# In-place weight forms of the 15-product scheme, handed out one operation at a time on GpSimd

## The chip, the cores and the metric

The kernel runs on one core of one Trainium2 chip. The metric is the device time of one execution in microseconds (us), as the median over runs. Each engine of the core takes its instructions in its own order: TensorE (PE in the profile) for matrix products, VectorE (DVE), ScalarE (ACT), GpSimd (POOL), and SyncE (SP), whose queue issues transfers. Engines wait for each other through semaphores.

## The reference

All data are float32. First an attention block: for each of 4 x 8 heads a state of 48 x 48 runs over 768 positions. Then its output, as 3072 rows of 384, goes through a gated feed-forward block:

```python
cur = einsum('bhd,bhe->bhde', u[None] * kt, vt)
y[:, :, t] = einsum('bhd,bhde->bhe', rt, state + cur)
state = w[None, :, :, None] * state + einsum('bhd,bhe->bhde', kt, vt)
...
g = x @ w_gate                               # (3072, 384) @ (384, 1536)
silu = g * (1.0 / (1.0 + exp(-g)))
return (silu * (x @ w_val)) @ w_out          # (3072, 1536) @ (1536, 384)
```

## The kernel before, in words

**Stages.** The attention block works on 24 tiles of 128 positions (six stretches of each of four batches). Its outputs, transposed, land in a ring of ten tiles, `xT`. The feed-forward block takes them in groups `g` of two tiles, and the hidden dimension of 1536 in 12 blocks `f` of 128. The first groups use plain products (`gate_value`, L444). Groups 2 to 7 are taken in pairs with `four` (L590): gate and value of a block, over two groups, come from eleven products of 128 x 128 by 128 x 256 in place of twelve. These use sums of weights made by `w_sums` (L576, five GpSimd operations for two blocks). Groups 8 to 11 are taken in pairs too, by `three_units` (L802), which handles three blocks (a triple `t`) at once with fifteen products.

**The forms.** The fifteen products of a triple need fifteen combinations ("forms") of its weights. Three are made in place, overwriting blocks of the weights `wgv`: `in_place` (L700) issues six GpSimd operations, two for each. A further six are made in other room by `w_forms` (L712), nine operations and a step `place` that names the room. As the weights are overwritten, a triple's in-place forms may begin only when the pair of groups 6 and 7, the last that uses them plainly (`g + 2 == THREES`, with `THREES` at 8), is done with those blocks.

**What sets the order.** All orders are written out by hand; instructions stand on each engine as the program emits them. `four_units` (L640) sorts the steps of a pair by a place, `11 * f - 5 + at`, and cuts them into 26 pieces. A block's steps are: PE products into two accumulator banks (`c_a`, `c_b`); ACT copies of the first bank at three points, named p1, u2 and u3 (L629); DVE sums and products with the second bank (L631 to L638); sigmoids on ACT (L602); and at the end, in step `h1`, one product on DVE (L605) and one on GpSimd (L606), which uses u3 and so gives its buffer back. The copies p1, u2 and u3 live in one ring of six buffers (tag `part`). As the program is built, p1 of block f + 3 takes the buffer that u3 of block f leaves: the copy of p1 on ACT waits for L606 three blocks earlier, and PE waits for the copy, because its next product is added onto the same bank.

`feed` (L872) draws these pieces between the steps of the attention tiles, in the loop of L1004. Each tile `s` brings to GpSimd `scale` (L301 and L304, written into `hats`) and `own_product` (L228 and L229), and at tiles past 12 also `move_blocks` (L349), 16 transfers on SP's queue which read `hats` and which the next tile's L304 has to wait for, and `turn_blocks` (L369), two transposes on DVE (L373) before them. `two_projections` (L656) gives the second product of the feed-forward block for a pair in 14 items; with the pair 6, 7 each item also calls `prepare_threes` (L774), which makes forms of triples 3, 1 and 0. Forms of triples 2 and 3 follow within `three_units`. After the last tile `x_forms` (L744) makes the corresponding sums of the inputs on DVE.

Of the kernel before, what the change touches and what calls it, by code (L numbers as in the profile page):

```python
# [22 lines left out]
def fast(  # L23
# [44 lines left out]
    dve, pool, act, pe, sp = nc.vector, nc.gpsimd, nc.scalar, nc.tensor, nc.sync  # L68
# [210 lines left out]
    for l in range(7):  # L279
        n = 1 << l  # L280
        f = pw[:, :, P - n : P - n + 1].to_broadcast([P, HP, n])
# [294 lines left out]
    def w_sums(g, f):  # L576

        (w11, w12, w13), (w21, w22, w23) = (
            [w[:, c, P * f : P * (f + 2)] for c in range(CC)] for w in (wg, wv)
        )  # L580
        t = three.tile([P, 5, 2 * P], FP32, name="s", tag="w_bits")
        x = part_of.setdefault(g, {})
        x["s", f] = x["s", f + 1] = t
        pool.tensor_add(t[:, 0], w21, w22)
        pool.tensor_sub(t[:, 1], t[:, 0], w11)
        pool.tensor_sub(t[:, 2], w22, t[:, 1])
        pool.tensor_sub(t[:, 3], w12, t[:, 1])
        pool.tensor_sub(t[:, 4], w13, w23)
# [51 lines left out]
    def four_units(g):  # L640

        steps = sorted((11 * f - 5 + at, f, what) for f in range(FC) for what, at in PLACE.items())
        pieces = [[] for _ in range(26)]
        n = 0
        for at, f, what in steps:
            k = max(n - 1, 0) if n < 4 else 3 + min(23 * (n - 4) // (11 * FC - 4), 22)
            if what == "p1" and f % 2 == 0 and f + 2 < FC:
                pieces[k].append(lambda f=f: w_sums(g, f + 2))
            k = (0, 1, 2, 2)[n] if n < 4 else k
            pieces[k].append(lambda f=f, what=what: four(g, f, what))  # L650
            if g + 2 == THREES and what == "h1" and f % 3 == 2 and f < 11:
                pieces[k].append(lambda f=f: in_place(f // 3))
            n += what[0] in "pc"
        return [lambda q=q: [do() for do in q] for q in pieces]

    def two_projections(g):  # L656

        def item(j, p):
            if g >= THREES and (j, p) == (0, 1):
                for do in wide.pop("last"):  # L660
                    do()
            if (j, p) in ((1, 0), (0, 1)):
                h_sums(g, p)
            elif (j, p) in ((1, 1), (0, 3)):
                h_sums(g + 1, p // 3)
            elif g + 2 < THREES:
                if (j, p) == (1, 2):
                    w_sums(g + 2, 0)
                elif (j, p) == (0, 6):
                    x_sums(g + 2)  # L670
            if THREES <= g + 2 < N // 2:
                prepare_threes(g + 2, order.index(f"{j}{p}"))
            project(g + j, p)
        order = "00 10 01 02 11 04 03 12 05 06 13 14 15 16".split()
        return [lambda j=int(o[0]), p=int(o[1]): item(j, p) for o in order]


    THREES = 8
# [19 lines left out]
    wide, todo_forms = {}, deque()  # L698

    def in_place(t):  # L700

        f = 3 * t
        w = [[wgv[:, :, c, P * (f + i) : P * (f + i + 1)] for c in range(CC)] for i in range(3)]
        for o, a, b, op in (
            (w[1][1], w[0][1], w[1][2], pool.tensor_add),
            (w[0][0], w[1][0], w[0][2], pool.tensor_add),
            (w[2][2], w[2][0], w[1][2], pool.tensor_sub),
        ):
            op(o, o, a)
            pool.tensor_sub(o, o, b)  # L710

    def w_forms(t):  # L712

        f = 3 * t
        made = wide["u", t] = {}

        w = [[wgv[:, :, c, P * (f + i) : P * (f + i + 1)] for c in range(CC)] for i in range(3)]
        def place():
            if t == 0:
                ring = three.tile([P, 6, 2, P], FP32, name="s", tag="w_bits")  # L720
                s = [ring[:, n] for n in range(6)]
            else:
                s = (early + spare)[6 * t - 6 : 6 * t]
                s = [x.rearrange("p (o t) -> p o t", o=2) for x in s]
            made.update(zip(("r2", "r3", "r13", "r11", "r5", "r9"), s))
            made.update({
                "r0": w[1][1], "r1": w[0][1], "r4": w[0][0], "r6": w[1][2], "r7": w[2][2],
                "r8": w[1][0], "r10": w[2][0], "r12": w[0][2], "r14": w[2][1],
            })

        def form(o, a, b, op):
            op(made[o], made[a], made[b])

        return [place] + [
            lambda x=x: form(*x) for x in (
                ("r2", "r14", "r6", pool.tensor_sub), ("r3", "r8", "r1", pool.tensor_sub),
                ("r13", "r12", "r10", pool.tensor_add), ("r9", "r2", "r13", pool.tensor_sub),
                ("r9", "r9", "r7", pool.tensor_sub), ("r5", "r3", "r13", pool.tensor_sub),
                ("r5", "r5", "r4", pool.tensor_sub), ("r11", "r3", "r2", pool.tensor_sub),
                ("r11", "r11", "r0", pool.tensor_add),  # L740
            )
        ]

    def x_forms(g):  # L744

        (x00, x01), (x10, x11), (x20, x21) = x_halves(g)
        lows2 = [two.tile([P, 3, 2, P], FP32, name="xf", tag="w_low") for _ in range(2)]
        v = [t[:, n] for t in lows2 for n in range(3)]
        v += [
            t[:].rearrange("p h d -> p (h d)")[:, 0 : 2 * P].rearrange("p (i t) -> p i t", i=2)  # L750
            for t in r_ld + k_ld
        ]
        last = two.tile([P, H, D], FP32, name="xf", tag="rk")
        v.append(
            last[:].rearrange("p h d -> p (h d)")[:, 0 : 2 * P].rearrange("p (i t) -> p i t", i=2)
        )
        v10, v14, v6, v13, v2, v12, d1, v3, v1, v8, v4 = v
        dve.tensor_add(v10, x01, x21)
        dve.tensor_add(v14, x10, x20)
        dve.tensor_sub(v13, x00, v10)  # L760
        dve.tensor_add(v12, v13, x20)
        dve.tensor_sub(d1, x11, x10)
        dve.tensor_sub(v2, d1, x20)
        dve.tensor_add(v6, v2, x21)
        dve.tensor_sub(v3, x00, x11)
        dve.tensor_sub(v1, x10, x00)
        dve.tensor_sub(v8, x01, x11)
        dve.tensor_sub(v4, x01, x00)
        wide["v", g] = {
            "r0": d1, "r1": v1, "r2": v2, "r3": v3, "r4": v4, "r5": x00, "r6": v6, "r7": x21,  # L770
            "r8": v8, "r9": x20, "r10": v10, "r11": x11, "r12": v12, "r13": v13, "r14": v14,
        }

    def prepare_threes(g, n):  # L774
        if g > THREES:
            if n == 10:
                x_forms(g)
            return
        if n == 1:
            in_place(3)  # L780
            todo_forms.extend(w_forms(1))
        if n == 7:
            todo_forms.extend(w_forms(0))
        for _ in range(2):
            if todo_forms:
                todo_forms.popleft()()
# [93 lines left out]
    def queue(g):  # L880
        if g == 0:
            todo.extend(
                (2 * f2 + 2 if j + f else 0, lambda j=j, f=f: gate_value(j, f))
                for f2 in range(FC // 2) for j in range(2) for f in (2 * f2, 2 * f2 + 1)
            )
        elif g % 2 and g > 1:
            first, *others = two_projections(g - 3)
            if g - 1 >= THREES:
                if g - 1 == THREES:
                    todo.extend((NW + 4, x) for x in others)  # L890
                return
            *pieces, last = four_units(g - 1)

            then = two_projections(g - 1)[0]

            for k in range(3):
                others.insert(len(others) - 3 + k, pieces.pop(0))
            pieces = ([first] if g == 3 else []) + others + pieces + [then, last]
            todo.extend((NW + 4, x) for x in pieces)
# [575 lines left out]
```

## Time and profile before

| what | value |
|---|---|
| median of three runs | 621.92 us (621.46 to 623.23) |
| the profiled execution: its time | 621.22 us |
| its span | 619.5 us |
| PE busy | 601.7 us, 97% of the span |
| DVE, POOL, ACT busy | 396.8, 324.7, 234.7 us |
| granted clock of PE | 0.999 |
| in-place forms (L709 and L710) | 24 operations, the first at 372.8 us, the last at 429.2 us |
| one of them | 0.72 to 1.45 us, most 0.73 to 0.76 |
| other forms (L732) | 36 operations from 429.8 to 487.7 us |

The span runs from the first to the last recorded instruction on the core; the execution's own time is 1.7 us more, with what lies around it. Starts in a timeline are microseconds from the span's start. A line such as "L606" is a line of the kernel; what stands left of an arrow is written, what stands right is read; "[3.58 <-POOL hTs L606]" means that the engine was idle for 3.58 us until that instruction released it.

### The profile page before, as it was taken

The numbers are of one execution on the slowest core, as the hardware profiler recorded it, in microseconds if no ns is written. First come the engines' busy times: TensorE is split into PE (matmuls) and PEld (weight loads), VectorE is DVE, ScalarE is ACT, GpSimd is POOL, SyncE is SP. The second block draws the span as 40 slices with busy tenths as digits, with TensorE's granted clock in tenths as the row PEclk, the third lists the DMA queues.
The fourth block names the chain that finished last, engine by engine and source line by source line (L and its number), as shares of the span: only waits on it lengthen the run. The fifth ranks groups of instructions, "written<-read, shape, count | busy, mean of one in ns | idle before, by whom it ended". The sixth has DMA issues, their size and how long they took to land.

```text
span 619.5 us, 12800 instructions
## 1 busy us (share of the span) xinstructions
PE 601.7 (97%) x4992; PEld 541.5 (87%) x4992; DVE 396.8 (64%) x749; ACT 234.7 (38%) x599; POOL 324.7 (52%) x366
## 2 busy tenths in 40 slices
PE   8799999999999999999999999899999999999996
PEld 7588888899888899988899988789988889988896
DVE  6878997364556564556658365659368875478770
ACT  3368786322343522244331334342223331133310
POOL 4789788944638423664633847957725610012200
PEclk9999999999999999999999999999999999999999
DMA  7989882343331203322221502022000000100001
GB/s 174 227 212 248 238 280 46 64 70 62 73 66 26 44 10 69 74 47 40 44 44 37 114 3 46 16 39 31 26 26 2 0 1 12 40 1 1 2 2 55
DMA packets 138006, 40.45 MB, mean 65 GB/s; under 512 B 128592, under 2 KB 131792, under 8 KB 137936
## 3 DMA queue, kind: packets, MB, share of 16 engines
q1 hardware_dynamic: 134480, 34.82, 26.4%
q10 hardware_dynamic: 3456, 4.72, 2.2%
q8 instruction: 41, 0.67, 0.5%
q14 instruction: 29, 0.24, 0.1%
HBM read 28.51 MB, written 4.72 MB: 54 GB/s over the span
## 4 chain that ended last, share of the span: by engine, by line
PE 78%; POOL 7%; SPq 3%; DVE 3%; DMA 2%; issue 1%; ACT 1%; DVEq 0%; POOLq 0%; ACTq 0%
PE o_f L522 13%; PE c_b L622 10%; PE c_l L797 10%; PE c_a L622 9%; PE o_a L522 8%; PE gv L448 7%; PE o_b L522 6%; PE y_ps L411 4%; PE c_y L797 3%; PE c_n L797 3%; SPq L358 3%; PE s_ps L381 3%; POOL wgv L216 1%; DMA hats<-hats 1%; POOL hTs L606 1%
## 5 line engine op out<-in xcount | busy, mean ns | idle before, releaser
L448 PE MATMUL gv<-xT,wgv 128*128 128x256 f32 x288 | 66.8, 385 | 0.6 <-ACT xT L415 0.6
L322 ACT ACTIVATE At<-ident,du 128x128 f32<-128x128 f32 x176 | 61.0, 396 | 15.2 <-DVE o_sb L536 7.2
L622 PE MATMUL c_b<-xT,wgv 128*128 128x256 f32 x216 | 64.5, 380 | 0.0
L821 POOL TENSOR_TENSOR At<-At,hats 128x512 f32<-128x512 f32 x8 | 10.2, 1272 | 97.9 <-ACT At L820 97.9
L448 PEld LDWEIGHTS gv<-xT,wgv 128*128 128x128 f32 x288 | 53.3, 190 | 8.8 <-ACT xT L415 0.9
L606 POOL TENSOR_TENSOR hTs<-hTs,u 128x256 f32<-128x256 f32 x36 | 27.9, 774 | 51.3 <-DVE hTs L605 51.0
L622 PE MATMUL c_a<-t,s 128*128 128x256 f32 x144 | 43.7, 385 | 2.9 <-ACT p L629 2.9
L622 PEld LDWEIGHTS c_b<-xT,wgv 128*128 128x128 f32 x216 | 40.8, 190 | 5.3
L386 DVE COPY_PREDICATED At<-mask,s_ps 128x512 f32<-128x512 int32 x48 | 33.0, 741 | 18.0 <-PE s_ps L381 9.5
L629 ACT COPY u<-c_a 128x256 f32<-128x256 f32 x72 | 26.7, 370 | 45.8 <-PE c_a L622 44.4
L622 PE MATMUL c_a<-xT,wgv 128*128 128x256 f32 x144 | 42.9, 379 | 0.0
L602 ACT ACTIVATE sg<-hTs 128x256 f32<-128x256 f32 x72 | 29.9, 416 | 30.2 <-DVE hTs L631 21.4
L304 POOL TENSOR_TENSOR hats<-r_ld,scales 128x384 f32<-128x384 f32 x20 | 21.0, 1049 | 32.0 <-DMA hats<-hats 32.0
L622 PE MATMUL c_b<-xT,s 128*128 128x256 f32 x144 | 37.0, 379 | 0.0
L636 DVE TENSOR_TENSOR u<-u,c_b 128x256 f32<-128x256 f32 x36 | 15.0, 417 | 33.1 <-PE c_b L622 29.6
L411 PE MATMUL y_ps<-At,v_ld 128*32 128x128 f32 x768 | 34.9, 273 | 1.3 <-DVE At L386 1.3
L622 PEld LDWEIGHTS c_a<-t,s 128*128 128x128 f32 x144 | 26.6, 190 | 7.6 <-ACT p L629 4.1
L411 PEld LDWEIGHTS y_ps<-At,v_ld 128*32 128x32 f32 x768 | 30.3, 110 | 2.4 <-issue 1.4
L631 DVE TENSOR_TENSOR hTs<-p,c_b 128x256 f32<-128x256 f32 x36 | 15.0, 417 | 24.8 <-PE c_b L622 22.3
L622 PEld LDWEIGHTS c_b<-xT,s 128*128 128x128 f32 x144 | 27.2, 190 | 3.9
L622 PEld LDWEIGHTS c_a<-xT,wgv 128*128 128x128 f32 x144 | 27.3, 190 | 3.5
L411 PE MATMUL y_ps<-rT,Z 112*32 112x128 f32 x480 | 29.8, 276 | 0.3 <-ACT kT L347 0.3
(241 smaller groups left out, 1528.3 us busy)
## 6 DMA issues: line engine op xcount, KB each, us to landing
hats<-hats SPq DMA_DIRECT2D x192, 32.0 KB, 2.0
w_bits<-in_moe_w_gate_dram SPq DMA_DIRECT2D x6, 768.0 KB, 6.7
v_ld<-in_v_dram SPq DMA_DIRECT2D x48, 96.0 KB, 3.3
w_bits<-in_moe_w_val_dram SPq DMA_DIRECT2D x6, 768.0 KB, 6.2
w_bits<-in_moe_w_out_dram SPq DMA_DIRECT2D x6, 768.0 KB, 6.4
out_dram<-o_sb ACTq DMA_DIRECT2D x24, 192.0 KB, 2.0
k_ld<-in_k_dram SPq DMA_DIRECT2D x20, 192.0 KB, 3.0
r_ld<-in_r_dram SPq DMA_DIRECT2D x20, 192.0 KB, 4.1
```

The source lines that it names most:

```text
L304: pool.tensor_mul(rhat_of(i)[:, :, 0:D], raw(i)[1], rscale)
L322: lambda h=h: act.activation(At[i % 2][:, h, :], ident[:], AF.Identity, scale=du[:, h : h + 1])
L358: sp.dma_start(out=bass.AP(tensor=dst.tensor, offset=dst.offset, ap=[list(dst.ap[0]), [-P, 2 * HP], [1, 32]],), in_=bass.AP(tensor=src.ten ...
L386: dve.copy_predicated(At[i % 2][:].rearrange("p (a e) t -> p a e t", e=2)[:, :, e], mask[:].bitcast(INT32).unsqueeze(1).to_broadcast([P, H ...
L411: pe.matmul(ps[32 * q : 32 * q + 32, cc, :], *x, start=start, stop=stop, skip_group_check=True,)
L448: pe.matmul(gv[:, o, :].rearrange("p (i t) -> p i t", i=2), wt[:, c, P * f : P * (f + 1)], xT[:, 2 * g % NX : 2 * g % NX + 2, c, :], start ...
L522: pe.matmul(ps, lhs[:, f, :], rhs[:, f, :], start=(f == 0 and n in (0, 1, 4)), stop=(f == FH - 1), skip_group_check=True,)
L602: act.activation(x[what, f][:], h[j], AF.Sigmoid)
L606: pool.tensor_mul(h[1], h[1], x.pop(("u3", f))[:])
L622: pe.matmul(ps.rearrange("p (i t) -> p i t", i=2), lhs, rhs, start=first, stop=what not in ("p2", "p5", "p4", "p3"), skip_group_check=True,)
L629: act.copy(x[nm, f][:], ps)
L797: pe.matmul(wide[chain][:, o].rearrange("p (i t) -> p i t", i=2), u[:, o], v, start=first and o == 0, stop=True, skip_group_check=True,)
```

## The change

`in_place` now returns its six operations as a list instead of issuing them, in the same order within each pair. For triples 0, 1 and 2 `four_units` gives each operation a place of its own: `11 * f + 20 + 5.4 * m` for the m-th of the triple that ends with block f, where all six stood behind `h1` of that block before (whose place is `11 * f + 19.5`). Two thus come to each following block. They go into the piece that the step ahead of them went to. For triple 3 the six go to the front of the list `todo_forms`, from which each item of the projections draws two, where all six were issued with item 1 before. Item 7 puts the forms of triple 0 ahead of what is left of triple 1's, where they followed it before.

The operations, their shapes and the buffers that they use stay as they are. The order of PE, DVE, ACT and SP stays as it is. On GpSimd, by the built order, L606 of blocks 2 to 11 of the pair stand in this row ("2x" are two in-place operations, "sums" one call of `w_sums`, "tile" L301, L304, L228 and L229 of one attention tile):

```
before: b2 6x b3 sums b4 b5 6x tile sums b6 L439 L439 b7 tile b8 6x b9 b10 b11 6x ...
after:  b2 2x b3 2x sums b4 2x b5 2x tile sums b6 1x L439 L439 1x b7 1x tile 1x b8 2x b9 2x b10 2x b11 6x ...
```

Another ring buffer changes hands: the copy of the first partial product of the projection (L530) now waits for L606 of block 9, for which the copy of its u2 (L530 too) waited before.

```diff
@@ four_units
         steps = sorted((11 * f - 5 + at, f, what) for f in range(FC) for what, at in PLACE.items())
+        if g + 2 == THREES:
+            steps += [
+                (11 * f + 20 + 5.4 * m, f, do)
+                for f in (2, 5, 8) for m, do in enumerate(in_place(f // 3))
+            ]
+            steps.sort(key=lambda x: x[0])
         pieces = [[] for _ in range(26)]
         n = 0
         for at, f, what in steps:
+            if not isinstance(what, str):
+                pieces[k].append(what)
+                continue
             k = max(n - 1, 0) if n < 4 else 3 + min(23 * (n - 4) // (11 * FC - 4), 22)
...
             pieces[k].append(lambda f=f, what=what: four(g, f, what))
-            if g + 2 == THREES and what == "h1" and f % 3 == 2 and f < 11:
-                pieces[k].append(lambda f=f: in_place(f // 3))
             n += what[0] in "pc"
@@ in_place
-        for o, a, b, op in (
-            (w[1][1], w[0][1], w[1][2], pool.tensor_add),
-            (w[0][0], w[1][0], w[0][2], pool.tensor_add),
-            (w[2][2], w[2][0], w[1][2], pool.tensor_sub),
-        ):
-            op(o, o, a)
-            pool.tensor_sub(o, o, b)
+        return [
+            lambda o=o, x=x, op=op: op(o, o, x) for o, x, op in (
+                (w[1][1], w[0][1], pool.tensor_add), (w[1][1], w[1][2], pool.tensor_sub),
+                (w[0][0], w[1][0], pool.tensor_add), (w[0][0], w[0][2], pool.tensor_sub),
+                (w[2][2], w[2][0], pool.tensor_sub), (w[2][2], w[1][2], pool.tensor_sub),
+            )
+        ]
@@ prepare_threes
         if n == 1:
-            in_place(3)
-            todo_forms.extend(w_forms(1))
+            todo_forms.extend(in_place(3) + w_forms(1))
         if n == 7:
-            todo_forms.extend(w_forms(0))
+            todo_forms.extendleft(reversed(w_forms(0)))
```

## The prediction

> **What bounds the kernel now.** I read the page's busy shares first. TensorE (PE) is busy 97% of a 619.5 us span and no other engine is above 64%, so a change on GpSimd (POOL) can only move the end through PE's idle time. The next view is the waits, of PE and of ScalarE (ACT), longest first; the columns are us in total, times, longest.
>
> ```profile
> PE c_a L622 <- ACT p L629: 2.9, 3, 2.2
> ACT p L629 <- POOL hTs L606: 7.4, 4, 3.6
> ```
>
> PE's longest wait anywhere is 2.2 us, for ACT's copy of p1 (L629). ACT in turn waited up to 3.6 us for L606, GpSimd's last step of a block. The timelines (start, us, engine, line) show that these are one event. ACT's:
>
> ```profile
> 396.01 0.37 ACT L629 COPY u<-c_a 128x256 f32<-128x256 f32 x1 [0.42 <-PE c_a L622]
> 396.37 0.42 ACT L602 ACTIVATE sg<-hTs 128x256 f32<-128x256 f32 x1
> 400.37 0.37 ACT L629 COPY p<-c_a 128x256 f32<-128x256 f32 x1 [3.58 <-POOL hTs L606]
> 401.54 0.37 ACT L629 COPY u<-c_a 128x256 f32<-128x256 f32 x1 [0.79 <-PE c_a L622]
> 403.26 0.37 ACT L629 COPY u<-c_a 128x256 f32<-128x256 f32 x1 [0.35 <-PE c_a L622]
> ```
>
> and PE's at the same moment:
>
> ```profile
> 397.97 0.59 PE L622 MATMUL c_b<-xT,wgv 128*128 128x256 f32 x2
> 400.80 0.70 PE L622 MATMUL c_a<-t,s 128*128 128x256 f32 x2 [2.24 <-ACT p L629]
> ```
>
> Counting blocks, the copy at 400.37 is p1 of block 9 of group pair 6 (the u at 396.01 is u3 of block 8, at 403.26 u3 of block 9). An undisturbed block takes 4.75 us from u3 to u3 (378.46, 383.21, 387.95 in the same timeline); here it took 403.26 - 396.01 = 7.25. So the wait costs PE 7.25 - 4.75 = **2.50 us**, a little more than the idle 2.24, because the pipeline restarts slowly.
>
> Why L606 was late is in the chain of waits, which leaves PE at 385.34 and comes back at 400.80:
>
> ```profile
> 386.20 0.73 POOL hTs L606
> 386.93 0.70 POOL wgv L709
> ...
> 391.66 0.97 POOL hats L301
> 392.63 0.97 POOL hats L304
> ...
> 395.63 0.70 POOL s L584
> ...
> 399.66 0.69 POOL hTs L606
> ```
>
> From L606 of block 5 to L606 of block 6 GpSimd never rests: six in-place forms, four operations for the attention tile, five weight sums, then L606. Ahead of it, at 382.98 to 386.20, it sat idle for 3.22 us, waiting for VectorE (DVE) to finish L605 of block 5.
>
> **What the Trainium skill says.** "Perfetto Trace Analysis", section "Optimization Strategy", says to take the gaps of the engine that counts and ask which semaphore ended each; this trace answers with the chain above. The same section reads a gap that repeats as too few buffers; here 2.2 of PE's 2.9 us on this wait are one gap, so it is one piece of queueing and not the ring of six in general. "SBUF — State Buffer", section "Who interferes with whom", says that a DVE instruction with two SBUF inputs and a GpSimd instruction that reads SBUF block each other. The trace agrees: L709 takes 0.72 to 0.73 us mostly, and 1.44 at 422.73, while DVE runs the sums of L495 to L499. "GPSIMD Engine Reference", section "3.1 Elementwise", gives 2.6 cycles per element for two inputs; for 256 elements at 1.2 GHz that is an estimate of 0.55 us before dispatch. The trace's 0.73 us is used.
>
> **The change, part by part.** Operations on GpSimd: 24 in-place and 36 other forms, the same before and after, of the same shape. Nothing is added or removed, on any engine or queue. Only the order in GpSimd's queue moves, and every other engine keeps its own order.
>
> *Triple 0.* Before, all six forms stood between L606 of blocks 2 and 3. Now two follow each of blocks 2, 3 and 4. After block 2's L606 (372.15) two forms end at 374.4; L606 of block 3 still waits for DVE's L605, about 376.6; two forms and five sums follow (two forms 1.5, five sums 4.06), so L606 of block 4 starts at about 382.9, where it was 382.25. P1 of block 7 needs it and is copied at 384.56: 0.9 us to spare. Two forms then run to 385.1, inside what was the idle 3.22 us, so L606 of block 5 stays at 386.20.
>
> *Triple 1.* Two forms follow block 5, in place of six: 386.88 to 388.39. Six took 391.62 - 386.88 = 4.74, two take 1.51, so all behind starts **3.23 us** sooner. The attention operations have their inputs, and the rows before and after show no wait on them in the queue. L606 of block 6 starts at 399.62 - 3.23 = 396.39 and ends at 397.1. The copy of p1 of block 9 follows u3 of block 8 by 1.35 us when nothing holds it (378.46 to 379.81), so at 397.36. PE can take it until 398.40 (397.97 plus the pitch of 0.43), thus a copy that starts up to 397.97. There is 0.8 us of spare: the wait goes, with all its 2.50 us.
>
> *The other four of triple 1* follow around L606 of blocks 6 and 7. Block 7's L606 starts at about 399.75 (form, two L439 of 1.15 together, form), and p1 of block 10 is due at 404.61 - 2.50 = 402.1. Hidden by 1.6 us.
>
> *Past the moves of hats.* One form comes ahead of L301, and one behind L229. L304 waits there for the 16 moves on SP's queue. They start at 397.32 on DVE's transpose of 396.59, which lies ahead of the stall and doesn't move; so this wait still ends at 409.35, while PE is 2.50 sooner. What is queued behind L304: L228, L229, one form, L606 of block 8, which ends at 409.35 + 0.95 + 1.08 + 0.96 + 0.75 + 0.75 = 413.85. ACT's u3 of block 11 waits for it and is due at about 413.4, so it is 0.3 to 0.5 late. PE wants that bank next for p4 of block 11, at 418.71 - 2.50 = 416.2, and the copy is done by 414.3: 1.9 us of cover. Then two forms and L606 of block 9 (416.1), which now releases the first projection's p1 copy, due at 418.54 - 2.50 = 416.04. If ACT is held there some tenths, next behind are diagonals and a sigmoid due at 418.6; the o_a bank itself is wanted at 424.7.
>
> *Triple 3 and the forms of triple 0.* Triple 3's six forms follow at two per projection, then five forms for triple 1, then all of triple 0's, then the last four. Triple 0's wait, as before, for the projection that ends at 441.1 (now 438.6), run 9 x 0.745 to 445.3, and are wanted at 458.39 - 2.50. The last four end at 448.3; GpSimd's next work waits for PE at 452.76 - 2.50 = 450.3. Cost nothing; cover 2.0 us.
>
> Sum: -2.50 us and nothing given back. The profiled execution, span 619.5 and time 621.22, would become 617.0 and 618.72. The median of the three runs, 621.92, stands 0.70 above that execution, so the median becomes **619.4**.
>
> The unknown is how much the forms and DVE stretch each other in the new overlaps. Low end: nothing, or a gain, since DVE's L605 of block 10 and two transposes hold PE 0.27 us at 415.80 and that could vanish (619.1). High end: the nine operations between 388.39 and 396.4 each take 0.91 for 0.73, as L588 did beside DVE: 9 x 0.18 = 1.6, so L606 ends 398.7, 0.8 past PE's limit (620.2). I take no stretch, because the same nine ran beside DVE work before and their 8.0 us already hold two stretched sums.
>
> **The rivals.** *A part is given back* (620.5): the stretch above, or later. DVE's x sums (L758 to L764) already hold PE 1.1 us at 457.45, because five of them take 0.84 to 0.96 beside GpSimd; if GpSimd's forms run 1.4 us longer than I have it, L758 and L759 stretch by 0.5 each too. *No change* (621.9): another release becomes the one that ends last. Nearest are p1 of block 7 (0.9 us) and u3 of block 11 (1.9 us); for it to hold, one estimate must be off by over 3 us, while PE, ACT and DVE otherwise keep their order. *Slower* (624): L606 of block 8 is held behind L304 while PE has moved on. It starts to cost once it ends after 415.75, 1.9 us later than worked out, and makes the kernel slower than before by 0.3% only past 415.75 + 2.50 + 1.87 = 420.1. For that the moves must land 6.3 us later than now; they have no new work ahead of them on SP. Against it: issue took 10.41 us and the wait ended 1.6 after.
>
> **How the numbers follow.** Forecast 74%, with its own range 618.6 to 620.2 (the low end above, and the scatter of the runs, 621.46 to 623.23, around their median); given back in part 12%; no change 8%; slower 6%. Of this kernel 0.3% is 1.87 us, about what its measurement tells from no change. The forecast clears that by 0.6 us, so I leave an eighth of it in "same", with most of the second case and all of the third: faster 0.68, same 0.26, slower 0.06. The range, 618.5 to 621.2, takes in the first two cases.
>
> **What would show it.** Right: PE's longest wait for p1 gone and its total for that pair near 0.7 us; ACT's copy of p1 of block 9 at about 397.4; six forms no longer in one run before about 420; L304 still ending its wait at about 409.3; the 1.1 us wait for L764 still there, 2.5 us sooner; span near 617.0. Wrong: a PE wait over 1 us for another copy between 384 and 420, L606 of block 6 later than 397.9, or a last wait at L764 grown to 2 us.

## The result, and the profile after

| | before | after |
|---|---|---|
| median of six runs each | 621.69 us (620.38 to 623.79) | 617.93 us (616.92 to 618.77) |
| the profiled execution: its time | 621.22 us | 618.37 us |
| its span | 619.5 us | 616.6 us |

The ratio is 0.9934, with a 95% interval of 0.9913 to 0.9956: 3.76 us less, where 2.5 had been forecast. The time fell just below the range, whose low end was 618.5. Repeated later, beside 27 runs of the kernel before on the same chip (median 620.98), it was 617.24 (617.04 to 618.45): 0.9946, 0.9929 to 0.9963, or 3.74 us less.

The waits of PE in the changed kernel, longest first (total, times, longest):

```profile
PE warm L263 <- POOL ident masks.py:199: 2.8, 1, 2.8
PE y_ps L411 <- DVE At L386: 1.4, 2, 1.2
PE c_l L803 <- DVE xf L771: 1.1, 1, 1.1
...
PE c_a L622 <- ACT p L629: 0.7, 2, 0.4
```

The wait of 2.2 us for the copy of p1 is gone from the pair in the last row; what is left of it is two of at most 0.4, in total the 0.7 that was forecast. The wait on DVE's x sums (L764 before, L771 now) is still 1.1. The queue that caused the old wait now reads so (GpSimd's timeline, changed kernel; start, us):

```profile
382.67 0.72 POOL L606 TENSOR_TENSOR hTs<-hTs,u 128x256 f32<-128x256 f32 x1
383.36 1.53 POOL L712 TENSOR_TENSOR wgv<-wgv 128x256 f32<-128x256 f32 x2
386.11 0.73 POOL L606 TENSOR_TENSOR hTs<-hTs,u 128x256 f32<-128x256 f32 x1 [1.22 <-DVE hTs L605]
386.80 1.53 POOL L712 TENSOR_TENSOR wgv<-wgv 128x256 f32<-128x256 f32 x2
388.28 1.01 POOL L301 TENSOR_TENSOR hats<-k_ld,scales 128x384 f32<-128x384 f32 x1
...
396.32 0.74 POOL L606 TENSOR_TENSOR hTs<-hTs,u 128x256 f32<-128x256 f32 x1
...
409.90 1.00 POOL L304 TENSOR_TENSOR hats<-r_ld,scales 128x384 f32<-128x384 f32 x1 [7.49 <-DMA hats<-hats]
...
413.83 0.73 POOL L606 TENSOR_TENSOR hTs<-hTs,u 128x256 f32<-128x256 f32 x1
```

The rows of L606 are blocks 4, 5, 6 and 8. Behind block 5 stand two forms (L712, the old L709 and L710) where there were six, and block 6 starts at 396.32 where it was 399.62. Triple 0's forms fill part of the idle time ahead of block 5: 1.22 us is left of 3.22. ACT's timeline, changed kernel, shows what that releases:

```profile
395.87 0.37 ACT L629 COPY u<-c_a 128x256 f32<-128x256 f32 x1 [0.42 <-PE c_a L622]
396.24 0.42 ACT L602 ACTIVATE sg<-hTs 128x256 f32<-128x256 f32 x1
397.22 0.37 ACT L629 COPY p<-c_a 128x256 f32<-128x256 f32 x1 [0.57 <-PE c_a L622]
398.89 0.37 ACT L629 COPY u<-c_a 128x256 f32<-128x256 f32 x1 [1.30 <-PE c_a L622]
400.62 0.37 ACT L629 COPY u<-c_a 128x256 f32<-128x256 f32 x1 [0.35 <-PE c_a L622]
...
414.59 0.37 ACT L629 COPY u<-c_a 128x256 f32<-128x256 f32 x1 [1.37 <-POOL hTs L606]
```

The copy of p1 of block 9 is at 397.22, in place of 400.37, and what ended the idle time before it is PE's own product, no longer GpSimd. From u3 of block 8 to u3 of block 9 it is 400.62 - 395.87 = 4.75 us, the undisturbed pitch.

**Where the time went, in the two traces.** Executions differ by 1 to 2 us before the change's place is reached: PE's wait for `kT` (L347) near 58 us ends anywhere between 57.65 and 59.57 in ten traces, and the copy of u3 of block 7 starts anywhere between 386.26 and 388.15, with the same work ahead of it on PE. So stretches are compared from one fixed event, the copy of u3 of block 7. Spans are known to 0.1 us, so a stretch to the end is good to 0.05.

| from u3 of block 7 to | before | after | difference |
|---|---|---|---|
| u3 of block 9 | 15.31 | 12.80 | -2.51 |
| the first o_a of the projections | 28.38 | 25.54 | -2.84 |
| the c_l behind the x sums | 69.50 | 66.65 | -2.85 |
| the end of the span | 231.55 | 228.78 | -2.77 |

The 2.51 is the wait. The next 0.33 comes at the end of the pair, where DVE held PE in the kernel before (its L605 of block 10 takes 0.75 us there and 0.42 in the changed kernel); PE's timeline of the kernel before,

```profile
415.09 0.60 PE L622 MATMUL c_a<-t,s 128*128 128x256 f32 x2
415.80 0.70 PE L622 MATMUL c_b<-t,s 128*128 128x256 f32 x2
```

and of the changed one:

```profile
412.45 0.59 PE L622 MATMUL c_a<-t,s 128*128 128x256 f32 x2
412.88 0.64 PE L622 MATMUL c_b<-t,s 128*128 128x256 f32 x2
```

The distance falls from 0.71 to the usual 0.43 us. The change need not be what does this: with the forms of triple 2 in one run as before, two traces below show 0.51 (projections alone) and 0.43 (wait filled), and with them spread one shows 0.64 (four ahead). Everything behind stays as it was, to 0.1 us. So the traces hold 2.8 us; the medians differ by 3.75. The remaining 0.9 to 1.0 us is no stretch of these two traces, and the experiments had to find it.

### The profile page after: what moved, and what is told of

Read it like the earlier page. It is cut to its first block, busy times and chain, and to the rows that moved or that the text cites. A ratio compares the mean times of both kernels' runs of the same rounds, so it can differ in the third digit from the quotient of the medians.

```text
span 616.6 us, 12802 instructions
## 1 busy us (share of the span) xinstructions
PE 601.6 (98%) x4992; PEld 541.4 (88%) x4992; DVE 395.5 (64%) x749; ACT 235.0 (38%) x599; POOL 325.4 (53%) x366
## 4 chain that ended last, share of the span: by engine, by line
PE 83%; DMA 4%; SPq 3%; POOL 3%; DVE 3%; ACT 2%; issue 1%; ACTq 0%; DVEq 0%; POOLq 0%
PE o_f L522 13%; PE c_b L622 11%; PE c_l L803 10%; PE c_a L622 10%; PE gv L448 8%; PE o_a L522 8%; PE o_b L522 6%; PE y_ps L411 5%; PE c_y L803 3%; PE c_n L803 3%; PE s_ps L381 3%; SPq L358 3%; DMA w_bits<-in_moe_w_gate_dram 1%; DMA w_bits<-in_moe_w_val_dram 1%; PE u_ps L426 1%
## 5 line engine op out<-in xcount | busy, mean ns | idle before, releaser
L606 POOL TENSOR_TENSOR hTs<-hTs,u 128x256 f32<-128x256 f32 x36 | 28.5, 791 | 48.6 <-DVE hTs L605 48.4
L304 POOL TENSOR_TENSOR hats<-r_ld,scales 128x384 f32<-128x384 f32 x20 | 21.2, 1061 | 33.0 <-DMA hats<-hats 33.0
L439 POOL TENSOR_TENSOR Z<-Z,w 48x192 f32<-48x192 f32 x32 | 18.7, 583 | 22.2 <-DVE Z L438 21.0
```

What stands on the lines that cost most here:

```text
L304: pool.tensor_mul(rhat_of(i)[:, :, 0:D], raw(i)[1], rscale)
L439: pool.tensor_mul(ze, ze, w)
L606: pool.tensor_mul(h[1], h[1], x.pop(("u3", f))[:])
```

## The experiments

The theory is the prediction's: six forms in one run ahead of block 6's L606 delay one copy, PE loses 2.5 us, and nothing else of the change counts. The first rival is that the gain comes from spreading in general: GpSimd's forms meet less of DVE's work, and the two stretch each other less. The second is that the other half of the change, the new order of the forms in the projections, has a part. The first four kernels ran beside 27 runs of the kernel before, median 620.82.

In the table the first two columns are the stretches of the table above, from each trace.

| kernel | u3 of block 7 to u3 of block 9 | to the end | median, us | ratio to before (95%) |
|---|---|---|---|---|
| before | 15.31 | 231.55 | 620.82, 620.98 | |
| spread alone | 12.80 | 228.68 | 617.40 | 0.9950 (0.9932 to 0.9969) |
| projections alone | 16.98 | 232.97 | 620.83 | 1.0003 (0.9993 to 1.0013) |
| one L606 on DVE | 12.80 | 228.84 | 616.93 | 0.9942 (0.9924 to 0.9960) |
| triple 1 alone | 12.81 | 228.65 | 617.29 | 0.9947 (0.9928 to 0.9966) |
| four ahead | 13.78 | 229.86 | 618.19 | 0.9959 (0.9942 to 0.9975) |
| x sums earlier | 12.81 | 227.85 | 616.43 | 0.9929 (0.9913 to 0.9945) |
| wait filled | 15.31 | 231.19 | 619.78 | 0.9984 (0.9976 to 0.9991) |
| after, again | 12.81 | 228.75 | 617.24 | 0.9946 (0.9929 to 0.9963) |

**The two halves of the change.** First the spread in `four_units` alone, with the projections' forms in the old order:

```diff
@@ prepare_threes, against the changed kernel
         if n == 1:
-            todo_forms.extend(in_place(3) + w_forms(1))
+            for do in in_place(3):
+                do()
+            todo_forms.extend(w_forms(1))
         if n == 7:
-            todo_forms.extendleft(reversed(w_forms(0)))
+            todo_forms.extend(w_forms(0))
```

> The forms of triples 0, 1 and 2 are spread as in the changed kernel; in the projections the six of triple 3 stand together with item 1 and triple 0's forms follow triple 1's, as before. Theory (PE waited 2.5 us for p1 of block 9, held by L606 of block 6 behind six forms): all of the gain is here, span about 616.6 like the changed kernel (before 619.5), no PE wait for p1 over 0.5 us. Rival (part of the gain beyond the 2.5 us forecast comes from the new order in the projections): span 617.0 or more, gain 2.5 or less.

Measured 617.40 (616.78 to 618.6). All of the gain is there without the projections' half. Then that half alone, all six forms of a triple right behind `h1` as before:

```diff
@@ four_units, against the changed kernel
                 (11 * f + 20 + 5.4 * m, f, do)
-                for f in (2, 5, 8) for m, do in enumerate(in_place(f // 3))
+                for f in (2, 5, 8) for do in in_place(f // 3) for m in (-0.08,)
```

> Only the order in the projections is new; the six forms of triples 0, 1 and 2 stand together behind blocks 2, 5 and 8, as before. Theory: no gain, span 619.5 give or take 0.3, PE's longest wait for p1 still 2.2 us. Rival (order in the projections gives the rest of the gain): 0.4 to 1.3 us faster than before with the 2.2 us wait still there.

Measured 620.83 in 22 runs (619.74 to 622.92): no difference from before, and the wait is where it was (2.2 us in its profile). The second rival falls: the projections' half is worth nothing. That the profile's span is 619.5, as expected, is luck: this execution comes to u3 of block 7 1.42 us sooner than the kernel before did, at 386.53, and then loses as much.

What it loses is what was missing from the sum. Its stretch across the wait is 16.98 us, 1.67 more than before. PE's timeline of this kernel:

```profile
396.54 0.59 PE L622 MATMUL c_b<-xT,wgv 128*128 128x256 f32 x2
399.37 1.22 PE L622 MATMUL c_a<-t,s 128*128 128x256 f32 x2 [2.24 <-ACT p L629]
400.39 1.06 PE L622 MATMUL c_b<-xT,wgv 128*128 128x256 f32 x2
401.24 1.80 PE L622 MATMUL c_b<-xT,s 128*128 128x256 f32 x4
402.88 0.59 PE L622 MATMUL c_a<-t,s 128*128 128x256 f32 x2
```

The wait is the same 2.24 us, but the eight matmul records behind it take 402.88 - 399.37 = 3.51 us, where the same eight take 402.63 - 400.80 = 1.83 in the kernel before. This is the 1.67. The windows over the stretch behind the wait say why. Columns are us, then the busy time of PE, PE's weight loads, DVE, ACT and POOL, then the granted clock; the last two are of the DMA engines. For this kernel

```profile
399.00:401.00 2.00, 1.63 (x4) 1.36 (x5) 0.00 (x0) 0.69 (x2) 1.85 (x4) 0.60 0.35 49
401.00:403.00 2.00, 2.00 (x7) 1.62 (x6) 0.42 (x1) 0.42 (x2) 0.71 (x1) 0.55 0.35 49
```

and for the stretch behind the wait in the kernel before, whose wait ends at 400.80 in its profiled execution:

```profile
400.70:402.00 1.30, 1.20 (x6) 1.08 (x7) 0.00 (x0) 0.42 (x2) 1.15 (x3) 1.00 0.33 45
402.00:405.00 3.00, 3.00 (x15) 2.65 (x14) 1.60 (x4) 1.78 (x6) 1.15 (x2) 1.00 0.35 50
```

After the wait the granted clock is 0.60 and 0.55 in one execution (0.50 if the window is put from 399.40 to 402.80) and 1.00 in the other, and PE's instructions are the same. So an execution can restart at half clock after this wait, and the one that the prediction was read from did not. Of the 27 runs of the kernel before, 17 have a mean granted clock of 0.997 or lower and a median of 621.24; the other 10 have 619.94. Of the 22 of this kernel, 13 have 621.36 and 9 have 619.94. A mean clock does not say where in an execution the clock fell; whether it is this wait is tested below. Where a kernel's executions split in this way its median is that of a mixture, and one profile shows one of the kinds.

**Is it the queue, or the overlap with DVE?** In the kernel before, with all six forms kept in one run, one operation is moved: L606 of block 6 goes to DVE.

```diff
@@ four, against the kernel before
-            pool.tensor_mul(h[1], h[1], x.pop(("u3", f))[:])
+            on = dve if (g, f) == (6, 6) else pool
+            on.tensor_mul(h[1], h[1], x.pop(("u3", f))[:])
```

> The kernel before with one operation moved: L606 of block 6 of the pair 6, 7 runs on DVE (about 0.42 us there), right behind its L605 near 391; GpSimd's queue keeps all forms in their old places. Theory: p1 of block 9 finds its buffer free, PE's wait of 2.2 us goes, gain 2.5 to 3.0, span 616.5 to 617.0. Rival (the gain is less blocking between DVE and GpSimd from spread forms, not that one wait): under 0.7 us, since all forms stand as before.

Measured 616.93 (616.82 to 617.78). On DVE the operation ends at 390.24 where it had ended at 400.34. This execution runs 1.69 us earlier (u3 of block 7 at 386.26 for 387.95), so that is 8.4 us sooner:

```profile
389.41 0.83 DVE L607 TENSOR_TENSOR hTs<-hTs,u 128x256 f32<-128x256 f32 x1
```

and ACT's copy of p1 of block 9 is no longer held (its timeline in this kernel):

```profile
395.61 0.37 ACT L630 COPY p<-c_a 128x256 f32<-128x256 f32 x1 [0.52 <-PE c_a L623]
```

One operation taken out of the queue gives as much as the whole change, within the scatter: 620.82 - 616.93 = 3.89 on the medians, which is more than the 2.5 to 3.0 expected, since these counted no half clock. GpSimd still runs the six forms back to back, 385.19 to 389.96, so the first rival falls too: what counts is which operation stands behind them. The 0.83 us may itself be a case of the stretch between the two engines, since DVE's L605, with the same shape and inputs of the same kind, takes 0.43 at 388.95 in this trace; it costs nothing there.

**Which of the triples.** Only triple 1 is spread; triples 0 and 2 stay together and the projections keep the old order.

```diff
@@ four_units, against the spread alone
-                (11 * f + 20 + 5.4 * m, f, do)
+                (11 * f + (20 + 5.4 * m if f == 5 else 19.568), f, do)
```

> Only triple 1's forms are spread (two behind each of blocks 5, 6 and 7 as in the changed kernel); triples 0 and 2 keep six together, and the projections their old order. Theory: all of the gain, span 616.6 to 617.0. Rival (spreading in general gives it): about a third of the gain, some 1 us, for one triple of three.

Measured 617.29 (616.82 to 618.46). Six operations of the 24 hold all of the gain; the other 18 are neutral. The spans of the three kernels that gain, 615.0, 615.1 and 615.3, lie 1.3 us and more below those expected, which were counted from the profile of the kernel before: these executions come to u3 of block 7 1.3 to 1.7 us sooner than that one. The stretches, not the spans, bear the comparison.

The second four ran beside another 27 runs of the kernel before: 18 with a granted clock of 0.997 or lower, median 621.28, and 9 with 619.88.

**How much of a delay costs how much.** Four forms of triple 1 ahead of block 6's L606 and two behind it, in place of two and four:

```diff
@@ four_units, against the changed kernel
-                (11 * f + 20 + 5.4 * m, f, do)
+                (11 * f + (20 + 5.4 * m if f != 5 else 20 if m < 4 else 31.2), f, do)
```

> The changed kernel, but four of triple 1's six forms stand ahead of block 6's L606 and two behind it. Theory (length of GpSimd's queue sets the wait): two forms more put L606 of block 6 1.5 us later than in the changed kernel, at an end near 398.6 for a copy that may start up to 397.7; PE waits 0.8 to 0.9 us for p1 of block 9. Time 0.7 to 1.0 us over the changed kernel. Rival (any wait there is enough to lose all): 2.5 us or more over it.

Measured 618.19 (617.95 to 618.75), 0.95 above the changed kernel beside it; the trace gives 0.97 across the wait and 229.86 - 228.75 = 1.11 to the end. GpSimd's timeline in this kernel:

```profile
385.51 3.01 POOL L712 TENSOR_TENSOR wgv<-wgv 128x256 f32<-128x256 f32 x4
...
396.50 0.91 POOL L606 TENSOR_TENSOR hTs<-hTs,u 128x256 f32<-128x256 f32 x1
```

ACT's and then PE's:

```profile
397.44 0.37 ACT L629 COPY p<-c_a 128x256 f32<-128x256 f32 x1 [2.06 <-POOL hTs L606]
```

```profile
397.86 0.70 PE L622 MATMUL c_a<-t,s 128*128 128x256 f32 x2 [0.71 <-ACT p L629]
```

The copy is 1.50 us later than it would be if nothing held it (u3 of block 8 is copied at 394.59, plus 1.35, is 395.94). By the prediction's figures such a copy could start up to 397.97 - 397.36 = 0.61 later without PE noticing, which leaves 0.89; PE's product starts 0.88 after it was due (397.86, for 396.55 + 0.43), of which 0.71 show as idle. So the slack is real, and past it the delay passes to PE one for one; another 0.1 is a slower first pair (0.54 for 0.43). The 0.14 more to the end go with a hold of DVE's at the end of the pair (0.64 for 0.43). The windows show a clock of 1.00 behind this short wait, and all six runs had 0.998 or more.

**Does the half clock belong to the wait?** In the kernel before, nine matmuls of 128 x 128 by 128 x 128 that nobody reads are put where PE waits. This adds work and takes none out.

```diff
@@ four, against the kernel before
         ps = x[acc, f]
+        if (g, f, what) == (6, 9, "p6"):
+            warm(9)
```

> The kernel before with nine matmuls of 128x128 on the identity, which nobody reads, put on PE ahead of p6 of block 9, so into its 2.2 us wait; GpSimd's queue as before. Theory (half of the executions of the kernel before pay some 1.3 us more, as PE restarts at half clock after this wait): the 2.50 us stay lost, but no execution restarts slowly; times gather near 619.9, the quick ones of the kernel before, granted clock 0.998 or more, median 0.7 to 1.2 us below the kernel before. Rival (the spread of the kernel before has another cause): same median as before, same spread, clocks of 0.996 in over a third of the runs.

Measured 619.78 in 22 runs (619.32 to 621.24). PE's timeline in this kernel:

```profile
397.42 0.59 PE L624 MATMUL c_b<-xT,wgv 128*128 128x256 f32 x2
397.85 2.17 PE L263 MATMUL warm<-ident 128*128 128x128 f32 x18
400.25 0.70 PE L624 MATMUL c_a<-t,s 128*128 128x256 f32 x2 [0.23 <-ACT p L631]
```

The copy is as late as ever and PE's own product still starts 2.4 us late; the stretch across it is 15.31, as before. But only 2 of 22 runs have a clock below 0.998, against 18 of 27, and the median falls by 620.98 - 619.78 = 1.20 us, to that of the executions of the kernel before at full clock (619.88). That is the missing term, and it is gone although the wait for the copy is not. The rest of the gain, 619.78 - 617.24 = 2.54, is the wait, for which the traces have 2.51. (In this profile DVE's hold of 0.3 us at the end of the pair is absent too, which is why its stretch to the end is 231.19 and not 231.55; up to that much of the 1.20 may be the hold and not the clock.)

**The next wait.** In the changed kernel the chain of waits has 0.84 us of DVE's xf (L771) ahead of the c_l of the first triple. DVE's x sums are moved ahead of the last of the projections' sums (L536), for which they had stood in line:

```diff
@@ the loop over the tiles, against the changed kernel
-        gaps(s, 4)
         if s == 24:
             x_forms(THREES)
+        gaps(s, 4)
```

> The changed kernel with the x sums of group 8 issued ahead of DVE's last sum of the projection instead of behind it (same operations). Theory (PE's next longest wait, 1.1 us for the last of them, is only their place in DVE's queue): the wait goes, 0.9 to 1.1 us faster than the changed kernel, best of all. Rival (GpSimd's forms stretch them wherever they stand, or o_b's bank comes late): 0.3 us or less, or a new wait for c_l.

Measured 616.43 (616.16 to 617.87), the lowest of all; 0.81 below the changed kernel beside it. That is a little less than the 0.9 to 1.1 expected, and the intervals of the two ratios overlap, so the times alone do not show it; but the 1.1 us wait is gone from the trace, and from u3 of block 7 to the end it takes 227.85 for 228.75, which is 0.90 less. DVE's timeline in this kernel:

```profile
445.46 0.35 DVE L539 TENSOR_TENSOR o_sb<-u,o_b 128x192 f32<-128x192 f32 x1 [3.48 <-PE o_b L522]
445.73 0.51 DVE L765 TENSOR_TENSOR xf<-xT 128x256 f32<-128x256 f32 x1
...
449.68 0.42 DVE L771 TENSOR_TENSOR xf<-xf,xT 128x256 f32<-128x256 f32 x1
...
452.96 0.34 DVE L536 TENSOR_TENSOR o_sb<-u,o_b 128x192 f32<-128x192 f32 x1
```

The sums go into the 3.48 us in which DVE had waited for PE, and L771 is done well ahead of its use; L536 comes 4 us later than in the changed kernel (452.96 for 448.95) and no wait on it shows. In this profile PE lost time in the start-up: 2.1 us to a wait for the load of `v_ld` that ends at 17.75, with a clock of 1.00 behind it, and up to 1.7 to a half clock behind two later waits for loads. PE's timeline and windows of this execution:

```profile
25.03 0.66 PE L343 MATMUL tp<-ident,hats 128*128 128x128 f32 x4 [1.54 <-DMA hats<-in_k_dram]
26.23 0.92 PE L343 MATMUL tp<-ident,hats 128*128 128x128 f32 x4 [0.55 <-DMA hats<-in_r_dram]
```

```profile
23.00:26.40 3.40, 1.31 (x9) 0.70 (x8) 2.55 (x5) 1.41 (x5) 3.21 (x4) 1.00 1.20 178
26.40:29.80 3.40, 3.40 (x56) 2.85 (x58) 1.85 (x4) 0.26 (x1) 2.02 (x3) 0.50 1.21 301
```

(The 1.7 is an estimate: half of the 3.40 us at a clock of 0.50.) That is why its span is 616.0 in spite of the shorter stretch, and its mean clock, 0.995, has nothing to do with p1 of block 9; the other five runs, none of them below 0.998, have a median of 616.38.

**The changed kernel again,** beside these:

> The changed kernel again, beside the others on one chip. Theory: median 3.2 to 3.6 us below the kernel before, of which 2.8 are the wait and the small one of DVE behind it, and the rest slow restarts that it no longer has; 617.0 to 617.6 if the kernel before stands at 620.8. Rival (the larger difference of the first comparison, 3.8, was the true one): 3.7 or more.

Measured 617.24 (617.04 to 618.45), with all six clocks at 0.998 or more. The time is as expected; the difference, 3.74, lies past the 3.2 to 3.6 and on the rival's side of 3.7, but its interval, 2.3 to 4.4 us by the ratio's, does not tell the two apart.

## Why the prediction was right or wrong

**Right, and shown: the place and the mechanism.** The gain is one copy that six forms delayed. L606 of block 6 starts at 396.32 (forecast 396.39), the copy at 397.22 (397.36), and the stretch across is 2.51 us shorter (2.50). Moving one operation away gives the same, and so do six of the 24 forms alone. Two readings beside it were not right. The 2.2 us were not PE's longest wait anywhere: that is 2.8 us at the start, for GpSimd's `ident`, in the changed kernel too. And that 2.50 is more than the idle 2.24 is for the most part no slow restart: a pair's record of 0.59 us outlasts its pitch of 0.43, which hides 0.16 of the delay, and only 0.10 is a slower first pair (401.33 - 400.80 = 0.53).

**Right: nothing is given back on the way.** Triple 0: L606 of block 4 at 382.67 (382.9), block 5 at 386.11 (386.20), its two forms inside what had been idle. Block 7 at 400.03 (399.75). L304's wait ends at 409.90, forecast 409.35: it did not move with PE, and is later as the issue of the moves took 11.11 us for 10.41. L606 of block 8 ends at 414.56 for 413.85, as L228 took 1.25 us and L304's wait ended 0.55 late; ACT sat idle for 1.37 us ahead of the copy of u3 of block 11 at 414.59, more than the 0.3 to 0.5 forecast, and PE shows no wait on it. The forms in the projections cost nothing, as the spread alone and the projections alone show. The assumption of no stretch held in the sum, not in each row: the nine operations ahead of block 6's L606 take 396.32 - 388.28 = 8.04 us, where they took 8.00, but L304 and L228 are now the long ones (1.19 and 1.20 for about 1.0) and the last two sums the short ones (0.73 and 0.74 for 0.91 and 0.90). The 1.1 us wait for DVE's x sums is still there.

**Wrong in size: "so the wait costs PE 2.50 us".** This term of the sum is the cost in one execution at full clock. In a good half of the executions, by their mean clock, PE also restarts at half clock behind it. That costs 1.67 us across the wait in the one trace that shows it (1.42 to the end, as DVE's hold is shorter there), and 1.3 to 1.4 us by the two sets of runs (621.24 - 619.94, 621.28 - 619.88). On the median it is 620.98 - 619.88 = 1.10. With it the sum is

- the wait, by the traces: 15.31 - 12.80 = 2.51
- what filling the wait takes away, on the median: 1.20, the half clock with up to 0.3 of DVE's hold
- together 3.71, where 3.74 and 3.76 were measured.

The 0.3 us of DVE's hold had been named as the low end. It is gone in the changed kernel's profile, but as it comes and goes in other traces whatever the forms do, that is not shown to be the change's work.

**Wrong in kind: "the median stands 0.70 above that execution".** It was taken as a fixed offset and carried over to the changed kernel. It was no such thing: the profiled execution of the kernel before was one at full clock that ran late (u3 of block 7 at 387.95, where six of the ten traces have 386.26 to 386.65), while some two thirds of the executions of that kernel, in both sets of 27, show the lower clock. In the changed kernel the median of six is 0.44 below its profiled execution, which ran late too (387.82). The offset held part of what the change removes, so keeping it kept that part out of the gain. This is the same miss seen from the other side: the forecast, 619.4, was 1.47 too high, of which 0.35 is in the profiled pair (618.37 for 618.72) and 0.70 + 0.44 = 1.14 in the offset.

**The rivals.** "A part is given back" and "no change" ended on the wrong side; "slower" would have needed L606 of block 8 to end past 415.75, and it ended 1.2 us short of that.

**What stays open.** In the first comparison the clocks of the kernel before are on record for its profiled execution only, so how much of those 3.76 us is half clock cannot be counted; the split is read from the later sets. Three of the six runs of the changed kernel there had a granted clock of 0.995 (618.77, 618.2 and 617.52, against 618.37, 617.66 and 616.92 for the others). No trace shows where in those runs the clock fell. The profile of the x sums earlier, with the same 0.995, has it in the start-up, as shown above, so a low mean clock alone does not point to this wait: of the 58 later runs of kernels in which the wait is gone, short or filled, five are at 0.997 or lower. And which executions restart at half clock, the traces don't tell: the 2.24 us wait is the same in both kinds.

## What to carry to other kernels

When a trace shows one wait on the engine that sets the end, look for the one operation that is late, and for what stands ahead of it in its queue; moving that one, or what is ahead of it, was worth as much here as reordering everything. Do not price a wait of PE at its idle time alone: the 2.24 us here cost 1.1 to 1.2 us more on the median for the clock behind it. Look at the granted clock behind the wait and at the clocks of all runs, since one profile shows only one kind. Do not carry an offset between a profiled execution and a median over to the changed kernel unless it is known what makes it.

## What the runs showed of the hardware

PE's granted clock fell to 0.50 for 3.4 us (399.40 to 402.80) after an idle time of only 2.24 us, in the one execution whose trace shows it (projections alone); by their mean clock, some of which may have another cause, 17 and 18 of 27 runs of the kernel before did the like. The Trainium skill, "TensorE: Matmul & The Clock Gate", section "HAM oscillation — how this bites in real kernels", gives as the rule "no PE-idle gaps >~3.4µs", and the section "What's actually happening" a full idle window of about that length for a fall to half clock. The half clock itself agrees with the trace; the length doesn't: 2.24 us was enough here, though not each time. In the start-up of the x sums earlier even two waits of 1.54 and 0.55 us, with 0.66 us of work between them, came before 3.4 us at 0.50, while one of 2.07 us in the same execution, and one of 1.99 in the changed kernel's second profile (ended at 25.01), have a clock of 1.00 behind them. So the length of a single wait does not decide it in these traces. The page calls the window free-running, so that where it starts differs between executions; that would fit a fall in some of them only, but no run here tests it. The wait of 0.71 us in four ahead, and that of 1.1 us for L771 in the changed kernel's profile, show a clock of 1.00 in the windows behind them.
